# Loading w_out two rows per descriptor, and reading the gate and value weights with a column step of two, in a convolution + SwiGLU kernel

## The chip, the cores and the metric

The kernel runs on one core of a Trainium2 chip. The metric is the device time of one execution in microseconds (us). A profiled execution also has a span, from its first to its last instruction, which is about 1.8 us shorter than the reported time.

## The reference

A causal convolution with seven taps per head (softmax of the given weights), then a SwiGLU feed-forward block:

```
x: 8 x 4096 x 192, weight: 8 heads x 7 taps           # 32,768 tokens in all
w = softmax(weight)
y[b,s,h,:] = sum_k w[h,k] * x_pad[b,s+k,h,:]           # 24 channels per head
g = y @ w_gate ; v = y @ w_val                         # 192 -> 1536
out = (g * sigmoid(g) * v) @ w_out                     # 1536 -> 192
```

## The kernel before

Tokens are handled in 64 blocks of 512. A block has 12 steps `j`. A step computes 128 of the 1,536 columns of gate and of value (three 64-row slices `k` of the 192 channels; gate from partitions 0 to 63, value from partitions 64 to 127; in the profile the two matmuls of a pair start within 0.01 us of each other around 400 us), then ScalarE makes silu and VectorE the product `h`. After every third step TensorE does a batch of down matmuls with `h` and `w_out`.

The weights are in one tile, slice by slice, and come in three groups of loads in the order of their columns. Each group is three DMAs: all gate slices, value slices 0 and 1, value slice 2.

```python
w16 = wpool.tile([P, SL, Dff], fp16, ...)       # 128 partitions, 3 slices, 1536 columns
wo16 = wpool.tile([P, NCH, D], fp16, ...)
def load_w(f0, f1):
    for half, src, i0, i1, s0 in ((0, moe_w_gate, 0, SL, 0),
                                  (1, moe_w_val, 0, SL - 1, 1), (1, moe_w_val, SL - 1, SL, 0)):
        seq(nc.gpsimd.dma_start(out=w16[Q * half : Q * half + Q, i0:i1, f0:f1], in_=src[...]))
...
xe_load(0)                  # first x tile
load_w(0, 384)
load_w(384, 1024)
xe_load(1)                  # second x tile
load_w(1024, Dff)
load_wo(0, 6); load_wo(6, NCH)
...
def gate_val(n):            # step n = block b, columns j
    for k in range(SL):
        for half, o in ((0, g), (1, v)):
            p0 = Q * half
            seq(nc.tensor.matmul(o, w16[p0 : p0 + Q, k, ts(j, P)], xc[b][k][p0 : p0 + Q, 0:TB], ...))
```

The Tile framework adds the semaphore waits, and goes by the part of a tile that is written or read: in the listing of the built program, below, slices of one tile wait for different loads. The kernel names none of the waits between weight loads and matmuls itself.

## Time and profile before

| | before |
|---|---|
| time, median | 793.2 us |
| span of the profiled run | 792.0 us |
| TensorE (PE) busy | 784.0 us, 99% |
| one gate and value pair | every 0.215 us |
| weight loads from `w` | 4,608, 94 ns each |

The page's busy table and its chain of work that ended last (shares of the span, first by engine, then by engine and source line), kernel before:

```profile
PE 784.0 (99%) x12018; PEld 493.9 (62%) x12018; DVE 584.1 (74%) x933; ACT 522.2 (66%) x910; POOL 67.4 (9%) x93
PE 97%; DMA 1%; POOL 1%; DVE 0%; ACT 0%; issue 0%; POOLq 0%
```

The groups by shape, kernel before: source line, engine, operation, what it reads, shape, count, then busy us, mean ns of one, and the idle time just before with what ended it. PEld is the weight load, which runs beside the matmuls (493.9 us of loads and 784.0 us of matmuls in a span of 792.0 us).

```profile
L545 PEld LDWEIGHTS <-w 64*128 64x128 f16 x4608 | 221.0, 94 | 212.7 <-issue 1.2 <-DMA w<-in_moe_w_val_dram 0.5
L545 PE MATMUL gate<-xc,w 64*128 64x512 f16 x2304 | 539.2, 376 | 0.0
L469 PEld LDWEIGHTS <-band 64*32 64x32 f16 x960 | 10.1, 91 | 4.9 <-issue 4.7
```

Then the timeline of TensorE near the start, kernel before (start us, duration us, engine, line, what; idle time in brackets). The first line is the last work on the first x tile, `cv` at 14.50 is the convolution of the second x tile:

```profile
9.70 0.33 PE L438 MATMUL turn<-ident,tme 128*128 128x128 f16 x3
9.97 0.39 PE L545 MATMUL gate<-xc,w 64*128 64x512 f16 x1
9.97 0.39 PE L545 MATMUL val<-xc,w 64*128 64x512 f16 x1
10.34 0.37 PE L545 MATMUL gate<-xc,w 64*128 64x512 f16 x1
...
14.50 0.72 PE L380 MATMUL cv<-xe,wide 64*64 64x48 f16 x63 [0.56 <-DMA xe<-in_x_dram]
```

Last, the timeline in the middle of the run, where down matmuls (`acc`) hand over to gate matmuls, kernel before:

```profile
399.80 0.91 PE L571 MATMUL acc<-wo,h 64*128 64x192 f16 x18
...
400.46 1.69 PEld L545 LDWEIGHTS <-w 64*128 64x128 f16 x18
400.54 0.38 PE L545 MATMUL gate<-xc,w 64*128 64x512 f16 x1
400.55 0.38 PE L545 MATMUL val<-xc,w 64*128 64x512 f16 x1
400.76 0.38 PE L545 MATMUL gate<-xc,w 64*128 64x512 f16 x1
```

The gate matmul starts 0.08 us after its weight load starts, though the load takes 94 ns. So it is at all 253 such returns in this trace: the matmul starts 80 to 81 ns after its load.

### The profile page before, as it was taken

Reading aid. Unit: us, or ns where it says so; the run is one execution under the profiler, and the core shown is the slowest. Engines: PE = TensorE matmul, PEld = TensorE weight load, DVE = VectorE, ACT = ScalarE, POOL = GpSimd, SP = SyncE. Lnnn points to the kernel's source line nnn. Section 1 sums busy time; section 2 is a strip of 40 time slices with the busy share of each in tenths; the row PEclk is TensorE's granted clock in tenths of the full one; section 3 lists DMA queues with packets and bytes.
Section 4 is the critical chain, followed back from the end, with each engine's and each line's share of the span. In section 5 each row is a group of like instructions: output and inputs, shape, how many; then the busy total and the mean of one; then the engine's idle time right before and its main releaser. Section 6 shows DMA issues by size and latency. Waiting matters only on the chain.

```text
span 792.0 us, 28590 instructions
## 1 busy us (share of the span) xinstructions
PE 784.0 (99%) x12018; PEld 493.9 (62%) x12018; DVE 584.1 (74%) x933; ACT 522.2 (66%) x910; POOL 67.4 (9%) x93
## 2 busy tenths in 40 slices
PE   8999999999999999999999999999999999999997
PEld 4666666666666666666666666666666666666665
DVE  7677777777777867767777777777777777777775
ACT  5676766666666666757666666666667667676664
POOL 8111010010100101001010000100001010000000
PEclk9999999999999999999999999999999999999999
DMA  9999577786857778567894769858587794726311
GB/s 131 149 204 146 125 116 118 164 124 146 105 120 152 129 147 119 120 126 125 155 140 113 117 112 165 128 133 118 112 154 121 150 115 118 136 81 116 80 42 42
DMA packets 214961, 99.23 MB, mean 125 GB/s; under 512 B 148776, under 2 KB 213936, under 8 KB 213936
## 3 DMA queue, kind: packets, MB, share of 16 engines
q1 hardware_dynamic: 167424, 78.75, 49.3%
q0 software_dynamic: 47136, 18.45, 21.7%
q8 instruction: 94, 1.54, 0.8%
q14 instruction: 35, 0.29, 0.1%
q10 hardware_dynamic: 272, 0.20, 0.1%
HBM read 36.90 MB, written 41.16 MB: 99 GB/s over the span
## 4 chain that ended last, share of the span: by engine, by line
PE 97%; DMA 1%; POOL 1%; DVE 0%; ACT 0%; issue 0%; POOLq 0%
PE gate L545 61%; PE acc L571 32%; PE cv L469 2%; PE val L545 1%; DMA xe<-in_x_dram 1%; POOL w L162 0%; POOL xe L97 0%; PE acc L592 0%; PE cv L380 0%; PE turn L438 0%; DVE h L556 0%; ACT sig L554 0%; DVE o_sb L627 0%; DVE tm L486 0%; ACT o_sb L731 0%
## 5 line engine op out<-in xcount | busy, mean ns | idle before, releaser
L556 DVE TENSOR_TENSOR h<-sig,val 128x512 f16<-128x512 f16 x768 | 507.7, 687 | 195.4 <-PE val L545 192.9
L554 ACT ACTIVATE sig<-gate 128x512 f16<-128x512 f32 x768 | 458.5, 597 | 234.9 <-PE val L545 207.4
L545 PE MATMUL val<-xc,w 64*128 64x512 f16 x2304 | 539.1, 376 | 0.2 <-DVE tm L486 0.2
L545 PE MATMUL gate<-xc,w 64*128 64x512 f16 x2304 | 539.2, 376 | 0.0
L545 PEld LDWEIGHTS <-w 64*128 64x128 f16 x4608 | 221.0, 94 | 212.7 <-issue 1.2
L571 PEld LDWEIGHTS <-h 64*128 64x128 f16 x6096 | 257.8, 94 | 66.0 <-issue 6.1
L571 PE MATMUL acc<-wo,h 64*128 64x192 f16 x6096 | 298.8, 243 | 0.0
L97 POOL DMA_DIRECT2D x<-in_x_dram x40 | 31.6, 792 | 437.0 <-ACT sig L554 429.9
L486 ACT CAST tm<-cv 128x480 f16<-128x480 f32 x60 | 30.6, 562 | 22.1 <-PE cv L469 22.1
L486 DVE CAST tm<-cv 128x480 f16<-128x480 f32 x60 | 36.6, 652 | 2.6
L627 DVE COPY o_sb<-acc 128x384 f32<-128x384 f32 x63 | 34.7, 550 | 0.0
L497 POOL COPY tm<-tm 128x1280 f16<-128x1280 f16 x15 | 18.8, 1252 | 137.3 <-DVE tm L486 129.1
L626 ACT COPY o_sb<-acc 128x384 f32<-128x384 f32 x63 | 30.1, 478 | 0.0
L469 PE MATMUL cv<-x,band 64*32 64x240 f16 x960 | 18.2, 265 | 0.0
L469 PEld LDWEIGHTS <-band 64*32 64x32 f16 x960 | 10.1, 91 | 4.9 <-issue 4.7
L132 POOL MEMSET x<- 6x192 f16 x7 | 1.7, 248 | 59.7 <-PE cv L469 59.6
L97 POOL DMA_DIRECT2D xe<-in_x_dram x9 | 6.0, 692 | 0.4 <-issue 0.3
L643 PE MATMUL warm<-fill 128*128 128x512 f16 x9 | 4.2, 628 | 1.2 <-DVE fill L91 1.2
L398 ACT CAST tme<-cv 128x288 f16<-128x288 f32 x8 | 2.9, 401 | 2.5 <-PE cv L380 2.5
L380 PE MATMUL cv<-xe,wide 64*64 64x48 f16 (+1 forms) x256 | 3.2, 192 | 1.1 <-ACT wide L338 0.6
L380 PEld LDWEIGHTS <-wide 64*64 64x64 f16 x256 | 2.7, 108 | 2.5 <-ACT wide L338 1.1
L438 PE MATMUL turn<-ident,tme 128*128 128x128 f16 x45 | 3.3, 220 | 0.8 <-ACT tme L398 0.5
(53 smaller groups left out, 40.0 us busy)
## 6 DMA issues: line engine op xcount, KB each, us to landing
out_dram<-o_sb SPq DMA_DIRECT2D x63, 384.0 KB
scr<-tm SPq DMA_DIRECT2D x105, 130.0 KB
x<-x SPq DMA_DIRECT2D x28, 480.0 KB
x<-in_x_dram POOLq DMA_DIRECT2D x24, 480.0 KB, 9.4
x<-in_x_dram POOLq DMA_DIRECT2D x7, 468.0 KB, 7.4
xc<-scr SPq DMA_TRANSPOSE x180
scr<-tm SPq DMA_DIRECT2D x15, 104.0 KB
wo<-in_moe_w_out_dram POOLq DMA_DIRECT2D x2, 288.0 KB, 6.3
```

The costliest lines, as they stand in the source:

```text
L97: nc.gpsimd.dma_start(out=t[p0 + i0 : p0 + i1, w0 - at : w1 - at, :], in_=bass.AP(tensor=x_flat.tensor, offset=(t0 + size * w0 - pad + i0) ...
L380: nc.tensor.matmul(o[Q * c : Q * c + Q, at : at + w], wide[Q * r : Q * r + Q, a, h, :], xe[e][Q * r : Q * r + Q, c : 2 * G : 2, h * grp : ...
L469: nc.tensor.matmul(banks[r][32 * c : 32 * c + 32, t * w : t * w + w], band[Q * r : Q * r + Q, h, :], x16[u][Q * r : Q * r + Q, NG * c : NG ...
L486: eng(tm[u][:, NG * r : NG * r + NG, 2 * grp * hp : 2 * grp * hp + 2 * grp].rearrange("p g (t e) -> p g t e", t=2), banks[r][:, 0 : 2 * w] ...
L497: seq(nc.gpsimd.tensor_copy(tm[u][:, :, SL * Q : 4 * Q], tm[u][:, :, 0:Q]))
L545: nc.tensor.matmul(o, w16[p0 : p0 + Q, k, ts(j, P)], xc[b][k][p0 : p0 + Q, 0:TB], start=(k == 0), stop=(k == SL - 1),)
L554: silu[n] = seq(nc.scalar.activation(sg, g, AF.Silu)).ins
L556: seq(nc.vector.tensor_tensor(hj, sg, v, op=ALU.mult))
L571: nc.tensor.matmul(acc[b][bank][:, s, :], hj[p0 : p0 + Q, ts(2 * bank + s, P)], wo16[p0 : p0 + Q, j, :], start=(not second and j == 0 and ...
L626: seq(nc.scalar.copy(o_sb[:, 0:2, :], acc[b][0]))
L627: seq(nc.vector.tensor_copy(o_sb[:, 2:4, :], acc[b][1]))
L643: nc.tensor.matmul(warm, fill[:, 0:P], fill, start=True, stop=True, skip_group_check=True,)
```

## The change

The intent is fewer and longer descriptors for `w_out`: a partition takes two neighbouring rows (2 x 768 B) in one descriptor instead of two rows 128 apart. Then row 256m + 2p + e of `w_out` sits at partition p. The rows of `h` must match, so step j = 2m + e computes every second column, and TensorE reads its weights with a step of two. A pair of steps now spans 256 columns, so the first load is widened from 384 to 512 columns.

```diff
     def load_wo(c0, c1):
-                out=wo16[:, c0:c1, :],
-                in_=moe_w_out[P * c0 : P * c1, :].rearrange("(c p) d -> p c d", p=P),
+                out=wo16[:, c0:c1, :].rearrange("p (m e) d -> p m (e d)", e=2),
+                in_=moe_w_out[P * c0 : P * c1, :].rearrange("(m p e) d -> p m (e d)", p=P, e=2),
...
-    load_w(0, 384)
-    load_w(384, 1024)
+    load_w(0, 512)
+    load_w(512, 1024)
...
+        cols = 2 * P * (j // 2) + j % 2
-                        w16[p0 : p0 + Q, k, ts(j, P)],
+                        w16[p0 : p0 + Q, k, cols : cols + 2 * P - 1 : 2],
```

More of the change, by code (lines that the diff above doesn't have):

```diff
@@ L172, in load_wo @@
             nc.gpsimd.dma_start(
-                out=wo16[:, c0:c1, :],
-                in_=moe_w_out[P * c0 : P * c1, :].rearrange("(c p) d -> p c d", p=P),
+                out=wo16[:, c0:c1, :].rearrange("p (m e) d -> p m (e d)", e=2),
+                in_=moe_w_out[P * c0 : P * c1, :].rearrange(
+                    "(m p e) d -> p m (e d)", p=P, e=2
+                ),
             )
```

## The prediction

> **What bounds the kernel now.** TensorE's matmul stream. The busy table gives PE 784.0 of 792.0 us, the chain that ended last is 97% PE (gate matmuls 61%, down matmuls 32%), and the table of waits shows only about 3 us of PE waiting, all near the start. In the timeline around 400 us a gate and a value matmul (64x128 weights, 512 columns, one on each half of the rows) run as a pair every 0.215 us; 36 down matmuls take 1.49 us, 83 ns a pair. 2304 pairs x 0.215 = 496 us and 3048 x 0.083 = 252 us make nearly the whole span.
>
> **Removed.** Half the descriptors of the two w_out loads (288 KB each, issued at 11.6 us, 6.3 us to landing): 1,536 rows of 768 B become 768 of 1,536 B, of 47,136 packets on that queue. It may save 0.5 us of Pool's 1.68 us of issuing and 1 us of landing. None of PE's waits name w_out, and the first down matmul starts at 18.15 us right behind gate matmuls. Worth 0 on the chain.
>
> **Moved.** The first weight load grows from 384 to 512 columns: about 1 us later (a third more of a 4.5 us landing), delaying the first gate matmul (9.96 us) by up to 0.5 us. But PE waits 0.6 us for the second x tile at 14.50 us anyway, and the bytes ahead of that tile are unchanged (1,024 columns either way). The fourth step now has its weights in the first load, which should remove the small wait for value weights at 12.2 us. Net at 14.5 us: about 0, at most 0.3 us.
>
> **Added.** 4,608 weight loads read every second fp16 column. Within a gate stage there is room: a load takes 94 ns (groups by shape) and has a 215 ns slot. It matters at the 250-odd returns from down to gate matmuls (four per block, 64 blocks): there the timeline shows the weight load starting at 400.46 and the matmul at 400.54, so a longer load shows directly. Loads of 32 columns take 91 ns and of 128 columns 94 to 98[...].[...] No run here has a strided load yet. I expect 94 ns again, at worst 10 ns more: 250 x 10 ns = 2.5 us (estimate).[...]
>
> **Prediction.** 793.4 us, 8 in 10 between 791.5 and 798. Faster by over 2%: 0.01; within 2%: 0.91; slower by over 2%: 0.08.
>
> **What would show it.** Groups by shape: w loads still 94 ns, gate and value matmuls 376 ns. Timeline: pairs every 0.215 us, no gap between down and gate matmuls. DMA: 768 packets fewer on the software queue, nobody waiting for w_out. Start: first gate matmul up to 0.5 us later, the second x tile's matmuls still near 14.5 us.
>
> **What would make it wrong.** Strided weights read markedly slower: w loads well over 100 ns, with gaps at every return to gate matmuls; over 215 ns, gaps at every pair and far more than 2%. Or reading strided weights disturbs the moving operand: the pairs' spacing would grow.

The forecast's sum was 793.2 us now, plus 0 for what is removed, about 0 and at most 0.3 us for what is moved, and 0 and at worst 2.5 us for what is added; it was put at 793.4 us. No number in the text stands behind the 0.08 for slower by over 2%. The 0.5 us of issuing, the 1 us of landing, the 1 us of the first load and the 10 ns a load are my estimates.

## More of the kernel before

TensorE is the bound, in a steady stream. And at the start it runs a race with the loads: the second gate matmul follows the first after 0.37 us, and the next input that it has to wait for by more than 0.1 us is the second x tile.

## The result, and the profile after

| | before | after |
|---|---|---|
| time, median | 793.2 us | 799.49 us |
| all runs | 792.92 to 794.07 | 798.79 to 800.53 |
| span of the profiled run | 792.0 us | 798.7 us |

The ratio is 1.0079 (95% interval 1.0061 to 1.0096), 6.3 us longer. Here and below a ratio is the mean time of one kernel's fast runs over that of the other's of the same rounds, so it is not quite the ratio of the medians quoted. By the 2% rule the two are the same; but the loss is clear of noise, and outside the range that I had predicted.

The groups by shape, kernel after:

```profile
L548 PEld LDWEIGHTS <-w 64*128 64x128 f16 x4608 | 221.7, 94 | 219.3 <-DMA w<-in_moe_w_gate_dram 4.7 <-issue 4.2 <-DMA w<-in_moe_w_val_dram 0.5
L548 PE MATMUL gate<-xc,w 64*128 64x512 f16 x2304 | 541.9, 377 | 4.5 <-DMA w<-in_moe_w_gate_dram 4.5
```

The weight loads still take 94 ns: reading every second column costs nothing here. What is new stands at the end of the lines. Once in the run, TensorE waited 4.5 us for a load of gate weights. The timeline near the start, kernel after:

```profile
10.05 0.37 PE L548 MATMUL gate<-xc,w 64*128 64x512 f16 x1
10.05 0.39 PE L548 MATMUL val<-xc,w 64*128 64x512 f16 x1
14.89 0.61 PE L548 MATMUL gate<-xc,w 64*128 64x512 f16 x1 [4.45 <-DMA w<-in_moe_w_gate_dram]
15.47 0.60 PE L548 MATMUL val<-xc,w 64*128 64x512 f16 x1
15.47 0.61 PE L548 MATMUL gate<-xc,w 64*128 64x512 f16 x1
15.87 0.63 PE L548 MATMUL val<-xc,w 64*128 64x512 f16 x1
...
20.54 0.38 PE L548 MATMUL gate<-xc,w 64*128 64x512 f16 x1
...
21.06 0.73 PE L382 MATMUL cv<-xe,wide 64*64 64x72 f16 x64
```

The first gate matmul starts on time, at 10.05 us. The second, which needs slice 1 of the same columns, starts 4.84 us later. And then the matmuls take 0.6 instead of 0.38 us and the pairs come every 0.42 us until about 20.5 us. The convolution of the second x tile begins at 21.06 us, not at 14.

Which load did it wait for? The chain of waits, kernel after, start us, duration us, what:

```profile
3.43 5.06 DMA w<-in_moe_w_gate_dram
8.49 0.28 issue
8.77 6.08 DMA w<-in_moe_w_gate_dram
14.85 0.05 issue
14.89 0.61 PE gate L548
```

The first gate load was issued at 3.43 us and had landed at 8.49 us, in good time. The wait ended with a load issued at 8.77 us. That is the third group, columns 1,024 to 1,535. The first step needs none of them. (Pool had waited 0.49 us before it issued this load, until the first gate load had landed at 8.49 us: the two share a semaphore, see below. In the kernel before, the first gate load had landed before Pool came to the third, at 8.23 us.)

The slow matmuls are a matter of TensorE's clock. The table of stretches, first kernel before, then kernel after (stretch and its length, PE busy us with instructions, granted clock as a share of full speed, DMA share, GB/s):

```profile
10.00:15.00 5.00, 4.44 (x93) 1.00 1.29 178
15.00:20.00 5.00, 5.00 (x90) 1.00 1.51 177
```

```profile
10.00:15.00 5.00, 0.55 (x5) 0.87 1.31 184
15.00:20.00 5.00, 5.00 (x23) 0.50 1.42 184
20.00:25.00 5.00, 5.00 (x107) 0.95 1.58 189
```

"PE busy 5.00 of 5.00" looks perfect from 15 to 20 us after the change, but it holds only 23 gate and value matmuls; at 0.215 us a pair some 46 would fit. (The 90 instructions before include short matmuls of the convolution, so the counts do not compare directly.) The clock was granted at 0.50. In a finer table its mean is 1.00 from 13.4 to 13.6 us, 0.71 in the next 0.2 us and 0.50 after that: it falls near 13.7 us, 3.2 us after TensorE had stopped at 10.44 us. Pairs then come every 0.42 instead of 0.215 us, and full clock is back near 20.5 us (0.72 from 20.4 to 20.6 us, 1.00 in the next 0.2 us), 5.6 us after the work resumed. That the clock stays at 1.00 when TensorE has work in this time, a run below shows.

After that nothing differs. The middle of the run, kernel after:

```profile
400.68 1.69 PEld L548 LDWEIGHTS <-w 64*128 64x128 f16 x18
400.76 0.38 PE L548 MATMUL gate<-xc,w 64*128 64x512 f16 x1
```

I took the convolution of the third x tile (step 10) as a mark. From there to the end of the span it is 792.0 - 22.37 = 769.6 us before and 798.7 - 28.95 = 769.8 us after. So of the 6.7 us of span that were lost, 6.6 us lie in the first 29 us.

The built programs say why. This listing of instructions with their waits is not a measurement. For the first step (a gate and a value load for each slice), `S3`, `S4`, `S5` are the semaphores of the first group's three DMAs; `S6`, `S7` those of the second group; the third group uses `S3` and `S4` again, so a second wait on these is for the third group:

```
                 before        after
slice 0, gate    S3            S3
slice 0, value   S4            S4
slice 1, gate    -             S6, S3 (again)
slice 1, value   -             S7, S4 (again)
slice 2, gate    -             -
slice 2, value   S5            S5
```

The changed program makes slice 1 wait for the second and third groups. In a partition, slice 1's first columns lie at elements 1,536 to 1,790. The third group's gate load runs from element 1,024 (slice 0, column 1,024) to 4,607 (slice 2, column 1,535), with holes. Taken from end to end, that range covers slice 1's columns, although the load writes none of them. Slice 0 (elements 0 to 254) lies before the range and does not wait. My theory: with a strided read, the overlap is judged by end-to-end address ranges, and the result is a wait for data that the matmul does not use; with a contiguous read it is judged exactly.

### The profile page after: what moved, and what is told of

Read it like the earlier page. It is cut to its first block, busy times and chain, and to the rows that moved or that the text cites. A ratio compares the mean times of both kernels' runs of the same rounds, so it can differ in the third digit from the quotient of the medians.

```text
span 798.7 us, 28592 instructions
## 1 busy us (share of the span) xinstructions
PE 786.7 (99%) x12018; PEld 494.5 (62%) x12018; DVE 584.4 (73%) x933; ACT 522.7 (65%) x910; POOL 67.5 (8%) x93
## 3 DMA queue, kind: packets, MB, share of 16 engines
q0 software_dynamic: 46368, 18.45, 21.8%
## 4 chain that ended last, share of the span: by engine, by line
PE 97%; DMA 1%; DVE 0%; POOL 0%; ACT 0%; issue 0%; POOLq 0%
PE gate L548 61%; PE acc L574 32%; PE cv L471 2%; PE val L548 2%; DMA w<-in_moe_w_gate_dram 1%; PE acc L595 0%; POOL xe L97 0%; PE cv L382 0%; PE turn L440 0%; DVE h L559 0%; ACT sig L557 0%; DVE o_sb L630 0%; DVE tm L488 0%; ACT o_sb L734 0%; POOL jid L186 0%
## 5 line engine op out<-in xcount | busy, mean ns | idle before, releaser
L440 PEld LDWEIGHTS <-tme 128*128 128x128 f16 x45 | 2.6, 98 | 1.9 <-issue 1.3
```

The costliest lines, as they stand in the source:

```text
L440: nc.tensor.transpose(bank[:, g, :], tme[b][:, g, Q * k : Q * k + P], ident)
```

## The experiments

Theory: the extra waits are the whole loss, partly as idle time and partly by the clock that falls in it. Rivals: the larger first load comes late; reading with a step is slow; the new `w_out` load disturbs something.

### The change with the old load sizes

```diff
-    load_w(0, 512)
-    load_w(512, 1024)
+    load_w(0, 384)
+    load_w(384, 1024)
```

> The change with its load sizes undone (384, 640, 512 columns again), strided reads and two-row w_out loads kept. Theory (the strided read of slice 1 is made to wait for the second and third weight load, which it does not need): the second gate matmul still starts only when the third gate load has landed, near 14.4 us (issued about 8.2 us, since the smaller first load lands sooner, plus 6 us), total 798.5 to 799.5 us. Rival (the larger first load is what comes late): first steps run from 10 us as before, 793 us.

Measured: 800.69 us, ratio 1.0091 (1.0074 to 1.0108). The second gate matmul started at 15.09 us, since the third gate load, issued at 8.15 us, took 6.89 us to land. I had put 6 us and a start near 14.4 us, 0.7 us too early; the time is 1.2 us above the range that I gave. The load sizes are not the cause: undone, the loss stays.

### The load sizes alone

```diff
 # on the kernel before
-    load_w(0, 384)
-    load_w(384, 1024)
+    load_w(0, 512)
+    load_w(512, 1024)
```

> The kernel before with the new load sizes alone (512, 512, 512), contiguous reads, old w_out load. Theory: no wait for the third load; first gate matmul near 10.0 us, second x tile's matmuls near 14.5 us, total 793.2 us within 0.5. Rival (the larger first load is to blame): 799 us.

Measured: 793.28 us, ratio 0.9997 (0.9982 to 1.0012). The second gate matmul started at 10.37 us. The larger first load is free; the rival falls from this side too.

### The change, weights stored load by load

```diff
 # on the kernel after
-w16 = wpool.tile([P, SL, Dff], fp16)
+w16 = wpool.tile([P, 3, SL, 512], fp16)
-    out=w16[Q * half : Q * half + Q, i0:i1, f0:f1],
+    out=w16[Q * half : Q * half + Q, f0 // 512, i0:i1, :],
-    w16[p0 : p0 + Q, k, cols : cols + 2 * P - 1 : 2],
+    w16[p0 : p0 + Q, cols // 512, k, cols % 512 : cols % 512 + 2 * P - 1 : 2],
```

> The change complete, but the weight tile stored load by load ([3 loads, 3 slices, 512 columns] per partition instead of [3 slices, 1536 columns]), so that no address range of one load spans columns of another. Reads are still strided by two. Theory: the extra waits are gone from the program, second gate matmul right after the first near 10.3 us, TensorE's clock never falls, weight loads 94 ns, total 793.2 us within 0.7. Rival (reading weights with a step of two is itself slow at the start or throughout): stays near 799 us.

Measured: 793.14 us, ratio 0.9995 (0.998 to 1.001), result correct. The built program's waits for the first step are again those of the kernel before. Weight loads and start, this kernel:

```profile
L548 PEld LDWEIGHTS <-w 64*128 64x128 f16 x4608 | 221.1, 94 | 212.7 <-issue 1.6
```

```profile
9.35 0.37 PE L548 MATMUL gate<-xc,w 64*128 64x512 f16 x1
9.35 0.39 PE L548 MATMUL val<-xc,w 64*128 64x512 f16 x1
9.79 0.37 PE L548 MATMUL gate<-xc,w 64*128 64x512 f16 x1
```

This has every part of the change: two-row loads, strided reads, new sizes. Only the order of the weights in memory differs, so that no load's end-to-end range covers another's columns. The loss is gone, and the wait with it. So neither strided reading nor the `w_out` load costs anything measurable; it also shows that the change could be had without the loss. It does not beat the kernel before: the interval contains 1.

### The kernel before with the waits alone

```diff
 # on the kernel before, contiguous reads, loads as they were;
 # w_loads lists the nine weight loads in the order of their issue
                 i = seq(nc.tensor.matmul(...))
+                if n == 0 and k == 1:
+                    for load in (w_loads[3 + half], w_loads[6 + half]):
+                        tc.add_manual_dep(i.ins, load.name, SYNC, reason="as after")
```

> The kernel before, contiguous reads and all loads untouched, with only the waits added by hand that the changed program has: slice 1 of the first step waits for the second and third gate and value loads. Theory: these waits are the whole cost, so second gate matmul near 14.5 to 15.1 us, half clock from about 13 to 20 us, 799 to 801 us as the run with the old sizes. Rival (strided reading or something else adds to it): clearly less than 799 us.

Measured: 800.82 us, ratio 1.0096 (1.0081 to 1.0111). The timeline and the stretches of this kernel:

```profile
9.37 0.39 PE L548 MATMUL gate<-xc,w 64*128 64x512 f16 x1
9.37 0.39 PE L548 MATMUL val<-xc,w 64*128 64x512 f16 x1
15.21 0.61 PE L548 MATMUL gate<-xc,w 64*128 64x512 f16 x1 [5.45 <-DMA w<-in_moe_w_gate_dram]
```

```profile
10.00:15.00 5.00, 0.00 (x0) 0.00 (x0) 0.00 (x0) 0.00 (x0) 3.17 (x6) 0.60 1.27 175
15.00:20.00 5.00, 4.76 (x21) 1.58 (x23) 1.69 (x3) 1.79 (x3) 3.96 (x6) 0.50 1.55 182
```

(In this view the columns after the stretch are the five engines' busy time, then the clock, 0.50.) This is the counterpart of the previous experiment: nothing of the change but its waits, and all of its loss. The built program's waits for the first step are those of the changed kernel. It also shows that the clock does not fall after one fixed idle time. TensorE worked from 8.32 to 9.76 us and stopped; if the clock fell once from 1.00 to 0.50, its mean of 0.60 from 10 to 15 us puts that near 11.0 us (an estimate from this mean), 1.2 us after TensorE had stopped; a fall 3.2 us after it would have given a mean of 0.80. In the changed kernel TensorE had worked about as long, from 9.05 to 10.44 us, and the clock fell 3.2 us after it had stopped. What decides the time, no run here shows.

### The change with the waiting time filled

Before slice 1 of the first step, 20 matmuls on a constant tile, whose result nobody uses:

```diff
         for k in range(SL):
+            if n == 0 and k == 1:
+                fillbank = apool.tile([P, TB], fp32, tag="acc0", name="fillbank")
+                for _ in range(20):
+                    seq(nc.tensor.matmul(fillbank, fill[:, 0:P], fill, start=True, stop=True, ...))
```

> The change with 20 idle matmuls (128x512, on a free bank) put between slice 0 and slice 1 of the first step, about 4.3 us of work, just to keep TensorE busy in its wait. Theory: the wait for the third load stays (second gate matmul near 14.9 us), but the 13 pairs after it run every 0.215 us instead of 0.425 us, so about 2.7 us of the 6.3 us come back: 796.8 us within 0.7. Rival (the slow matmuls from 15 to 20 us come from the strided reads or the DMA load, not from the idle time before them): 799.5 us.

Measured: 797.83 us, ratio 1.0056 (1.0041 to 1.0071). The timeline (its last line is a weight load) and, for 15 to 20 us, the table of stretches (columns as just explained):

```profile
10.34 4.49 PE L549 MATMUL fillbank<-fill 128*128 128x512 f16 x20
14.77 0.39 PE L557 MATMUL gate<-xc,w 64*128 64x512 f16 x1
15.11 0.39 PE L557 MATMUL val<-xc,w 64*128 64x512 f16 x1
15.11 0.39 PE L557 MATMUL gate<-xc,w 64*128 64x512 f16 x1
15.33 0.38 PE L557 MATMUL val<-xc,w 64*128 64x512 f16 x1
...
15.10 0.55 PEld L557 LDWEIGHTS <-w 64*128 64x128 f16 x8 [0.25 <-DMA w<-in_moe_w_val_dram]
```

```profile
15.00:20.00 5.00, 5.00 (x102) 2.47 (x103) 3.75 (x6) 3.84 (x8) 4.25 (x7) 1.00 1.48 192
```

The wait stayed: the third gate load landed at 14.4 us (8.24 + 6.2), just before the filling ended, and slice 1's value matmul at 15.11 us still had to wait for the third value load, as the last line shows. The clock did not fall (1.00 from 10 to 20 us, with TensorE busy for all of it), and the pairs came every 0.215 us. So the loss has two parts. What is left, 0.0056 x 793.6 = 4.4 us, is the wait. The clock's part is the difference to the changed kernel: 0.0023 of 793 us, 1.8 us, against the runs made first, or 0.0035, 2.8 us, against the kernel with the old sizes, which ran on the same chip in the same rounds. Neither is clean, since the third loads did not land at the same time: slice 1's value matmul starts at 15.11 us here, at 15.47 us in the changed kernel and at 15.71 us with the old sizes. From there to the second x tile it takes 3.20, 5.59 and 5.48 us (the tile at 18.31, 21.06 and 21.19 us), so by the profiled runs the clock's part is 2.3 to 2.4 us. I had expected 796.8 us within 0.7 and was 0.3 us off the edge: I had read 2.7 us from the profiled run of the change, which was its slowest (span 798.7; the others 796.9 to 798.0).

### The two-row w_out load alone

```diff
 # on the kernel before; rows of h and w_out no longer match, the result is wrong on purpose
-    ... .rearrange("(c p) d -> p c d", p=P)
+    ... .rearrange("(m p e) d -> p m (e d)", p=P, e=2)
```

> The kernel before with the two-row w_out load alone (wrong result on purpose: rows of h and w_out no longer match). Theory: worth nothing, 793.2 us within 0.7; 768 packets fewer on the software queue, Pool issues the two loads in about 1.5 instead of 1.7 us, no wait of TensorE names w_out. Rival (fewer descriptors help or hurt): a difference over 1 us.

Measured: 793.85 us, ratio 1.0005 (0.9988 to 1.0022). The software queue moved 46,368 packets instead of 47,136, 768 fewer as counted beforehand, Pool issued the two loads in 1.63 instead of 1.68 us, and no wait of TensorE named `w_out`. Issuing became 0.05 us shorter, where I had expected 0.2 us (and 0.5 us in the prediction), and the loads took 7.0 instead of 6.3 us to land, where the prediction had hoped to save 1 us. The part that the change was made for is worth nothing here, because nobody waits for it.

### A step of four

```diff
 # on the kernel stored load by load
-    cols = 2 * P * (j // 2) + j % 2
+    cols = j % 4
-    w16[p0 : p0 + Q, cols // 512, k, cols % 512 : cols % 512 + 2 * P - 1 : 2]
+    w16[p0 : p0 + Q, j // 4, k, cols : cols + 4 * P - 3 : 4]
 # and w_out with e=4, loads of 8 and 4 chunks
```

> The load-by-load storage with four w_out rows per partition and weights read with a step of four columns (8 bytes). Theory[...]: weight loads 94 ns, 793.1 us within 0.7. Rival (a longer step slows the weight read): weight loads clearly over 94 ns and gaps where down matmuls return to gate matmuls, at 20 ns each some 5 us more.

Measured: 793.4 us, ratio 1.0 (0.9985 to 1.0015). The time is as expected, the weight load is not (a reason that I had given for 94 ns is cut above, since no run shows it):

```profile
L548 PEld LDWEIGHTS <-w 64*128 64x128 f16 x4608 | 254.5, 110 | 183.4 <-issue 1.6
...
400.13 1.70 PEld L548 LDWEIGHTS <-w 64*128 64x128 f16 x18
...
400.21 0.38 PE L548 MATMUL gate<-xc,w 64*128 64x512 f16 x1
```

A step of four columns made each load 16 ns longer, and this cost no measurable time: the gate matmul starts 0.08 us after its load (lines two and three, from the timeline).

### A step of twelve

```diff
 # on the kernel after
-    w16[p0 : p0 + Q, k, cols : cols + 2 * P - 1 : 2]
+    w16[p0 : p0 + Q, k, j : j + 12 * P - 11 : 12]
 # and w_out with e=12, in one load
```

> All twelve w_out rows of a partition in one descriptor (9,216 B), weights read with a step of 12 columns (24 bytes[...]), old storage order. The first step now truly needs all three weight loads, so a start like the changed kernel's (first gate matmul near 14.5 us, 6 to 7 us lost). What is tested is the steady state: if the step is free, weight loads stay at 94 ns and the total is 799 to 801 us[...]. I hold the first likelier, at 60%.

Measured: 800.39 us, ratio 1.0088 (1.0073 to 1.0103). Here the first step needs all columns, so the wait at the start is real (first gate matmul at 14.20 us). The groups by shape and the middle of the run:

```profile
L546 PEld LDWEIGHTS <-w 64*128 64x128 f16 x4608 | 313.8, 139 | 138.7 <-DMA w<-in_moe_w_gate_dram 4.3 <-issue 4.2 <-DMA w<-in_moe_w_val_dram 0.4
```

```profile
400.27 0.66 PE L572 MATMUL acc<-wo,h 64*128 64x192 f16 x12
400.68 1.74 PEld L546 LDWEIGHTS <-w 64*128 64x128 f16 x18
400.76 0.38 PE L546 MATMUL gate<-xc,w 64*128 64x512 f16 x1
```

Neither branch of my expectation came true as written. (The second put the total at 810 us or more, with loads some 50 ns longer.) The loads grew by 45 ns, to 139 ns, but the total stayed at the level of the start's loss alone. The last lines show how: the gate matmul still starts 0.08 us after its weight load starts, the same as with loads of 94 ns. The next return looks the same (load at 403.61 us, gate matmul at 403.69 us), and in the whole run the gate matmuls had 4.1 us of idle time before them, all of it the one wait at the start. Why a longer step makes a load longer, no run here shows. The time from the mark at the third x tile to the end is 798.6 - 28.90 = 769.7 us, as in every kernel here.

### All runs side by side

The third column is when TensorE starts on slice 1 of the first step, the fourth when it starts the convolution of the third x tile, the last the time from there to the end of the span, all from the profiled run.

| kernel | time, median | slice 1 | third x tile | from there to the end |
|---|---|---|---|---|
| before | 793.2 | 10.34 | 22.37 | 769.6 |
| after | 799.49 | 14.89 | 28.95 | 769.8 |
| after, old sizes | 800.69 | 15.09 | 29.08 | 769.8 |
| sizes alone | 793.28 | 10.37 | 21.64 | 769.7 |
| after, stored load by load | 793.14 | 9.79 | 21.75 | 769.8 |
| before, waits alone | 800.82 | 15.21 | 29.48 | 769.7 |
| after, wait filled | 797.83 | 14.77 | 26.20 | 769.7 |
| w_out load alone | 793.85 | 10.58 | 22.04 | 769.8 |
| step of four | 793.4 | 9.76 | 22.02 | 769.8 |
| step of twelve | 800.39 | 14.79 | 28.90 | 769.7 |

The steady part is the same within 0.2 us everywhere. The differences of several us are settled by when slice 1 starts, and by the clock after it. Among the kernels without the wait the start still scatters by 0.7 us (21.64 to 22.37).

## Why the prediction was wrong

The measured 799.49 us lies above the predicted range of 791.5 to 798.

- *"What bounds the kernel now"* held: TensorE's stream, and its steady part did not change by more than 0.2 us.
- *"Removed. [...] Worth 0 on the chain"* was right: the two-row load alone gives a ratio of 1.0005.
- *"Moved. [...] Net at 14.5 us: about 0, at most 0.3 us"* is the step that failed. As far as the bytes go it was right: the larger first gate load landed at 8.49 us, the first gate matmul moved from 9.97 to 10.05 us, and the sizes alone cost nothing (0.9997). But I took for granted that each step waits only for the load that carries its columns. The changed program waits for two more loads, and the second x tile's matmuls began at 21.06 us instead of near 14.5.
- *"Added."* The load time was right for this change: 94 ns, at a step of two; with the passages cut, it stands as the author's estimate. The mechanism beside it was wrong. I said that at a return from down to gate matmuls "a longer load shows directly", and based the tail of the range on it. With loads of 110 and 139 ns the matmul still starts 0.08 us after the load does (400.13 to 400.21 us with a step of four, 400.68 to 400.76 us with twelve), and no time is lost (769.8 and 769.7 us from the mark to the end). In these traces a matmul begins before its weight load is complete: 80 ns against 139 ns with a step of twelve, and 80 to 81 ns against 94 ns at all 253 returns of the kernel before.
- *"What would make it wrong"* named slow strided loads and a disturbed moving operand. Neither occurred (loads of 94 ns, pairs every 0.215 us in the steady part). A new wait was not on the list, nor was the clock, which turned a wait of 4.4 us into a loss of 6.3 us.

What is shown and what is argued: that the extra waits are necessary and sufficient for the loss is shown, by taking them away with everything else kept but the order of the weights in the tile, and by adding them with nothing else changed. That they arise from judging strided reads by end-to-end ranges is inferred. It fits which of the six loads wait in the listing, and the storage order that removed them; I did not look further into it.

## What to carry to other kernels

When an access is changed from contiguous to strided in a framework that derives the waits, compare the waits in the built program before and after: a read may begin to wait for loads that it does not use. Storing the data so that each load fills one unbroken range of a partition removed such waits here at no cost (ratio 0.9995). The wait of 4.5 us on TensorE was paid for twice here, first as idle time and then at half clock (0.50 from 13.7 to 20.5 us); and saving descriptors of a load that nobody waits for saved nothing (ratio 1.0005).
